# One 8-row share of two load and store steps moved from DMA engines 6 and 7 to engines 14 and 15, on GpSimd's queue

## The chip, the cores and the metric

The kernel runs on one core of a Trainium2 chip. The metric is the device time of one execution in microseconds (us). Beside it there is a profile of one execution, with its trace: every instruction of the engines PE (TensorE), DVE (VectorE), ACT (ScalarE), POOL (GpSimd) and SP (SyncE), and every packet that the core's 16 DMA engines moved.

## The reference

The input x has the shape (1, 512, 512, 192) in bfloat16: 262,144 pixels of 192 channels. The channels form 4 groups of 48. The reference pads by k // 2, and k is 1, so there is no padding and the loop has one step:

```python
for i in range(k):
    for j in range(k):
        out = out + jnp.einsum('bhwgc,gcd->bhwgd', xg[:, i:i+H, j:j+W, :, :], w[i, j])
```

So each pixel's 48 channels of a group are multiplied by that group's 48 x 48 matrix. It is a 1x1 grouped convolution. Input and output have 100.66 MB each.

## The kernel before, in words

**Pieces.** The pixels are cut into pieces that each lie over the 128 partitions (rows) of the SBUF tensor `ring`. A full piece has `BIG` = 104 pixels (columns) in each of the 128 rows: 104 x 192 x 2 = 39,936 bytes in a row, contiguous in DRAM. `ring` has five slots of 104 columns. Slot 0 first takes four short pieces (`HEAD`, 8 to 32 columns). `plan_pieces` puts two *shared* pieces (`SHARED`) among the full ones, after five and after ten of them. A piece is loaded into its slot, computed, written back into the same place, and stored from there.

**Shared pieces.** A full piece is one DMA, whose 128 rows go to all 16 engines, 8 rows each. A shared piece is 72 columns wide, does not use all rows, and is made of *shares*, each a block of rows with its own DMA. The tuple of a share is (first row, rows, parts, columns, queue): `parts` is the outer size that the DRAM side of its DMA shows (`transfers`), and so the number of DMA engines that take part, with 4 rows each. Before, there are three shares:

- rows 0 to 31, 41 columns, 8 parts, by SP's (load) and ACT's (store) queue: engines 0 to 7
- rows 32 to 47, 72 columns, 4 parts, by the same queues: engines 0 to 3
- rows 52 to 95, 72 columns, 11 parts, by GpSimd's queue both ways: engines 5 to 15

A row of 41 columns has 15,744 bytes, one of 72 columns 27,648. All rows of the piece are computed on, also those that were not loaded; only the shares are stored.

**The cursor.** The two queues of SP and ACT begin each DMA at engine 0. In GpSimd's queue a DMA over fewer than 16 engines goes on at the engine after the last one used. So `pool_dmas` issues, ahead of each 11-part transfer, a small DMA over 5 engines into the scratch tensor `cur` (5 rows of 2 x 32 elements), so that the 11 parts fall on engines 5 to 15 and the turn ends at engine 16, which is 0.

**Order of the work.** There is no scheduler; every engine's program is written out by hand.

- SP issues all loads in order of the pieces. `wait_slot` makes it wait, before a load into a slot, until the stores of the piece five slots back have landed, those of ACT's queue (`st_sem`) and those of GpSimd's (`ps_sem`).
- PE takes groups of 4 columns (`columns(g)`), 526 in all, two to a pair: 12 transposes of 128 x 128 per pair into PSUM (`xT_ps`, L247), and 6 matmuls per group against the block matrix `wt` into `o_ps` (L262). Before the first group of a piece it waits for its load, of both queues.
- DVE copies the transposed pair to SBUF (L286). ACT copies each group's result from PSUM back into `ring` (L304), and issues a piece's stores when it has copied the first group behind it (`store`, L298). The last pieces are stored in parts.
- POOL builds the identity and selection matrices at the start. After that it only handles the two shared pieces: wait for the slot, cursor and load (L197, L199), wait for ACT to have finished the piece, cursor and store (L197, L199).

Of the kernel before, what the change touches and what calls it, by code (L numbers as in the profile page):

```python
# [6 lines left out]
BF16 = mybir.dt.bfloat16  # L7
# [23 lines left out]
SHARED_AT = (5, 11)  # L31
SHARED_COLS = 72
SYNC, POOL = 0, 1
SHARED = ((0, 32, 8, 41, SYNC), (32, 16, 4, SHARED_COLS, SYNC), (52, 44, 11, SHARED_COLS, POOL))
CURSOR = 5
NXP = 4
NXS = 3
NOB = 4
# [38 lines left out]
def plan_pieces(npix):  # L77
    few = sum(rows * cols for _, rows, _, cols, _ in SHARED)
    at = list(SHARED_AT)
    if npix < len(at) * few + 128 * (sum(HEAD) + BIG * (at[-1] + 2)):  # L80
        at = []
    cols = (npix - few * len(at)) // 128
    assert cols % 4 == 0
    head = list(HEAD) if cols >= sum(HEAD) + BIG else []
    mid = cols - sum(head)
    slots = [[(BIG, None)]] * (mid // BIG) + ([[(mid % BIG, None)]] if mid % BIG else [])
    for i in at:
        slots.insert(i, [(SHARED_COLS, SHARED)])
    if head:
        slots.insert(0, [(s, None) for s in head])  # L90
    pieces, g, pix = [], 0, 0
    for n, parts in enumerate(slots):
        c = n * BIG % RCOLS
        for s, shares in parts:
            pieces.append(Piece(len(pieces), n, c, g, s, shares, pix))
            c, g, pix = c + s, pieces[-1].g1, pieces[-1].pix_end
    assert pix == npix
    return pieces


def bass_standalone__grouped__vision_kernel(nc, x, w, out):
# [10 lines left out]
    xf = x.rearrange("b h w c -> (b h w) c")  # L112
# [6 lines left out]
    def transfers(ap, ring, p, queue, c0=0, c1=None):  # L119
        for b in p.on(queue):  # L120
            px = ap[b.pix:b.pix + b.rows * b.cols, :]
            e0, e1 = c0, min(c1 or b.cols, b.cols)
            if b.parts == 1:
                view = px.rearrange("(p i) n -> p (i n)", p=b.rows)[:, e0 * C:e1 * C]
            else:
                view = px.rearrange("(c a i) n -> a c (i n)", a=b.parts, c=b.rows // b.parts)
            yield view, ring[b.r0:b.r0 + b.rows, (p.at + e0) * C:(p.at + e1) * C]
# [10 lines left out]
    pooled = [p for p in pieces if p.on(POOL)]  # L138
    pool_val = {p: 16 * len(p.on(POOL)) for p in pooled}

    with ExitStack() as es:
        block = es.enter_context(nc.Block())
        ring = es.enter_context(nc.sbuf_tensor("ring", [128, RCOLS * C], BF16))
# [8 lines left out]
        def sem(name):  # L152
            return es.enter_context(nc.semaphore(name))
# [3 lines left out]
        pl_sem = {p: sem(f"pl{p.i}") for p in pooled}  # L157
        ps_sem = {p: sem(f"ps{p.i}") for p in pooled}
        cur_sem = sem("cur_sem")
        cur = es.enter_context(nc.sbuf_tensor("cur", [CURSOR, 2 * len(pooled), 2, 32], BF16))  # L160
        w_sem, id_sem, e_sem, wb_sem, wc_sem = (sem(s) for s in ("w_sem", "id_sem", "e_sem", "wb_sem", "wc_sem"))
        p0_sem, p1_sem = sem("p0_sem"), sem("p1_sem")
        t_done, mm_done = sem("t_done"), sem("mm_done")
# [7 lines left out]
        def wait_slot(wq, p):  # L171
            for q in pieces:
                if q.slot == p.slot - RCOLS // BIG:
                    wq.wait(st_sem[q.i], st_val[q])
                    if q in pl_sem:
                        wq.wait(ps_sem[q], pool_val[q])

        @block.gpsimd
        def _(gp):
            wq = Waiter(gp)  # L180
            gp.memset(esel[:], 1.0).then_inc(p0_sem, 1)  # L181
            gp.memset(ident[:], 1.0).then_inc(p1_sem, 1)  # L182
            gp.wait_ge(p0_sem, 1)
            gp.affine_select(out=esel[:], in_=esel[:], pattern=[[-1, ECOLS]],  # L184
                             compare_op=AluOpType.is_equal, fill=0.0, base=ESHIFT,
                             channel_multiplier=1).then_inc(e_sem, 1)
            gp.wait_ge(p1_sem, 1)
            gp.affine_select(out=ident[:], in_=ident[:], pattern=[[-1, 128]],  # L188
                             compare_op=AluOpType.is_equal, fill=0.0, base=0,
                             channel_multiplier=1).then_inc(id_sem, 1)  # L190
            turns = [0]

            def pool_dmas(p, ap, inward, done):
                for dram, sbuf in transfers(ap, ring, p, POOL):
                    n = turns[0]
                    few = xf[0:CURSOR, 0:128].rearrange("p (a b) -> p a b", a=2)[:, :, 0:32]
                    gp.dma_start(cur[:, n], few).then_inc(cur_sem, 16)  # L197
                    turns[0] += 1
                    gp.dma_start(*((sbuf, dram) if inward else (dram, sbuf))).then_inc(done, 16)  # L199

            for p in pooled:
                wait_slot(wq, p)
                pool_dmas(p, xf, True, pl_sem[p])
                wq.wait(fa_done, p.g1)
                pool_dmas(p, of, False, ps_sem[p])
            for p in pooled:
                wq.wait(ps_sem[p], pool_val[p])
            wq.wait(cur_sem, 16 * turns[0])
# [130 lines left out]
```

## Time and profile before

| | |
|---|---|
| runs | 486.94, 486.96, 487.05 us; median 486.96 |
| profiled execution, its time | 486.76 us |
| its span, first to last instruction | 485.0 us |
| PE / ACT / DVE / POOL busy | 436.1 / 396.6 / 252.6 / 5.9 us |
| granted TensorE clock, mean | 0.957 |
| DMA moved | 202.24 MB, 417 GB/s |
| GpSimd's shared loads, issue to landing | 24.3 us (median of 2) |
| GpSimd's shared stores, issue to landing | 26.5 us (median of 2) |

The span is 1.8 us shorter than the execution's time. Busy times are sums over the span, so an engine that is busy 90% can still wait for another. In the profile's list of DMA queues q1 is SP's queue (loads), q10 ACT's (stores), q0 GpSimd's, and q8 and q14 bring instructions from DRAM. The share of a queue is the time that its packets took, as a share of 16 engines' span.

### The profile page before, as it was taken

How to read it: one execution, taken by the hardware profiler on the slowest of the kernel's cores; microseconds unless marked ns; L12 is line 12 of the kernel's file. 1: busy time of each engine (PE TensorE's matmuls, PEld its weight loads, DVE VectorE, ACT ScalarE, POOL GpSimd, SP SyncE). 2: the span in 40 equal slices, each digit the busy share in tenths (PEclk: the TensorE clock that was granted, in tenths of full speed). 3: DMA queues.
4: the chain of work that ended last, by engine and by line, in shares of the span. 5: the costliest groups of instructions: out<-in, count | busy, mean ns of one | idle time of the engine just before them, and what ended most of it. 6: DMA issues, size and time to landing. Idle time of an engine off the chain costs nothing.

```text
span 485.0 us, 14084 instructions
## 1 busy us (share of the span) xinstructions
PE 436.1 (90%) x6322; PEld 397.3 (82%) x6322; DVE 252.6 (52%) x264; ACT 396.6 (82%) x527; POOL 5.9 (1%) x16
## 2 busy tenths in 40 slices
PE   5979999999998999699859998999999999999910
PEld 5878889889888988688859897898888899889800
DVE  2535555565655555255525654655655556565500
ACT  3949999999998999499848997999989999999920
POOL 1000000100000000000000000000000000000000
PEclk9979999999999999799979999999999999999965
DMA  8999999999999999999999999999999999999993
GB/s 325 443 440 409 426 447 408 397 428 433 433 421 449 408 430 437 441 424 420 431 439 419 427 428 421 420 422 421 428 430 417 430 432 421 430 421 431 422 423 151
DMA packets 8443, 202.24 MB, mean 417 GB/s; under 512 B 1361, under 2 KB 1361, under 8 KB 2001
## 3 DMA queue, kind: packets, MB, share of 16 engines
q1 hardware_dynamic: 3496, 98.25, 47.6%
q10 hardware_dynamic: 4440, 98.23, 47.6%
q0 software_dynamic: 448, 4.87, 2.4%
q8 instruction: 50, 0.82, 0.6%
q14 instruction: 9, 0.07, 0.0%
HBM read 100.68 MB, written 100.66 MB: 415 GB/s over the span
## 4 chain that ended last, share of the span: by engine, by line
PE 70%; DMA 22%; issue 1%; another core or an unknown queue 1%; ACT 1%; ACTq 0%; SPq 0%
PE o_ps L262 41%; PE xT_ps L247 29%; DMA ring<-in_x_dram 13%; DMA out_dram<-ring 9%; ACT ring L304 1%; ACTq L298 0%; SPq L217 0%; SPq L213 0%
## 5 line engine op out<-in xcount | busy, mean ns | idle before, releaser
L304 ACT CAST ring<-o_ps 128x768 bf16<-128x768 f32 x526 | 395.3, 802 | 66.4 <-PE o_ps L262 57.4
L286 DVE COPY xT_sb<-xT_ps 128x1536 bf16<-128x1536 bf16 x263 | 252.0, 958 | 205.3 <-PE xT_ps L247 205.3
L262 PE MATMUL o_ps<-wt,xT_sb 128*128 128x144 bf16 (+1 forms) x3156 | 295.6, 236 | 9.7 <-ACT ring L304 3.9
L262 PEld LDWEIGHTS o_ps<-wt,xT_sb 128*128 128x128 bf16 x3156 | 214.6, 99 | 47.2 <-ACT ring L304 33.7
L247 PE MATMUL xT_ps<-ident,ring 128*128 128x128 bf16 x3156 | 224.6, 222 | 14.3 <-DMA ring<-in_x_dram 14.2
L247 PEld LDWEIGHTS xT_ps<-ident,ring 128*128 128x128 bf16 x3156 | 193.7, 99 | 15.5 <-DMA ring<-in_x_dram 12.5
L197 POOL DMA_DIRECT2D cur<-in_x_dram x4 | 2.3, 584 | 286.3 <-DMA out_dram<-ring 160.0
L230 PE MATMUL o_ps<-w_sb,esel 48*128 48x48 bf16 x10 | 0.6, 209 | 2.8 <-DMA w_sb<-in_w_dram 2.8
L230 PEld LDWEIGHTS o_ps<-w_sb,esel 48*128 48x128 bf16 x10 | 0.5, 111 | 2.8 <-issue 2.8
L280 DVE CAST wt<-o_ps 128x480 bf16<-128x480 f32 x1 | 0.7, 657 | 3.4 <-PE o_ps L230 3.4
L304 ACT ACT_TABLE_LOAD x1 | 1.3, 1283 | 0.8 <-PEq L324 0.8
L199 POOL DMA_DIRECT2D ring<-in_x_dram x2 | 1.1, 564 | 0.0
L199 POOL DMA_DIRECT2D out_dram<-ring x2 | 1.1, 559 | 0.0
L184 POOL TENSOR_SCALAR_AFFINE_SELECT esel<-esel 48x272 bf16<-48x272 bf16 x1 | 0.4, 402 | 0.0
L181 POOL MEMSET esel<- 48x272 bf16 x1 | 0.3, 318 | 0.3 <-POOLq L324 0.3
L188 POOL TENSOR_SCALAR_AFFINE_SELECT ident<-ident 128x128 bf16<-128x128 bf16 x1 | 0.3, 283 | 0.0
L182 POOL MEMSET ident<- 128x128 bf16 x1 | 0.2, 197 | 0.0
L324 POOL MEMSET const-float32-0.0<- 128x1 f32 x1 | 0.1, 98 | 0.3 <-issue 0.3
L324 POOL MEMSET const-bfloat16-1.0<- 128x1 bf16 x1 | 0.1, 101 | 0.0
L324 POOL MEMSET const-uint8-127<- 128x1 uint8 x1 | 0.1, 101 | 0.0
L324 POOL MEMSET const-float32-1.0<- 128x1 f32 x1 | 0.1, 98 | 0.0
## 6 DMA issues: line engine op xcount, KB each, us to landing
ring<-in_x_dram SPq DMA_DIRECT2D x18, 4992.0 KB, 35.0
out_dram<-ring ACTq DMA_DIRECT2D x12, 4992.0 KB, 42.8
out_dram<-ring ACTq DMA_DIRECT2D x10, 2496.0 KB, 47.3
out_dram<-ring ACTq DMA_DIRECT2D x3, 1536.0 KB, 21.2
ring<-in_x_dram POOLq DMA_DIRECT2D x2, 1188.0 KB, 24.3
out_dram<-ring POOLq DMA_DIRECT2D x2, 1188.0 KB, 26.5
ring<-in_x_dram SPq DMA_DIRECT2D x1, 1536.0 KB, 11.2
ring<-in_x_dram SPq DMA_DIRECT2D x1, 1344.0 KB, 8.1
```

The lines of the kernel that those rows point to most:

```text
L181: gp.memset(esel[:], 1.0).then_inc(p0_sem, 1)
L184: gp.affine_select(out=esel[:], in_=esel[:], pattern=[[-1, ECOLS]], compare_op=AluOpType.is_equal, fill=0.0, base=ESHIFT, channel_multipli ...
L188: gp.affine_select(out=ident[:], in_=ident[:], pattern=[[-1, 128]], compare_op=AluOpType.is_equal, fill=0.0, base=0, channel_multiplier=1) ...
L197: gp.dma_start(cur[:, n], few).then_inc(cur_sem, 16)
L199: gp.dma_start(*((sbuf, dram) if inward else (dram, sbuf))).then_inc(done, 16)
L230: last = pe.matmul(o_ps[:, NOB - 1, col:col + CG], lhsT=esel[:, s0:s0 + 128], rhs=w_sb[:, g, :], start=True, stop=True, skip_group_check=True)
L247: last = pe.transpose(xT_ps[:, g % NXP, j * 128:(j + 1) * 128], xg[:, j * 128:(j + 1) * 128], ident[:])
L262: last = pe.matmul(o_ps[:, v % NOB, c0_:c1_], lhsT=xs[:, j * 128:(j + 1) * 128], rhs=wt[:, WOFF[tc]:WOFF[tc] + (c1_ - c0_)], start=(tc == ...
L280: dve.tensor_copy(wt[:], o_ps[:, NOB - 1, 0:WCOLS]).then_inc(wc_sem, 1)
L286: dve.tensor_copy(xT_sb[pair % NXS][:, 0:n * 2 * UC].rearrange("p (g c) -> p g c", g=n), xT_ps[:, b0:b0 + n, 0:2 * UC]).then_inc(e_done, 1)
L304: act.copy(dst, o_ps[:, v % NOB:v % NOB + 2, 0:UC]).then_inc(fa_done, 1)
L324: nc = _bacc.Bacc("TRN2", target_bir_lowering=False, num_devices=1)
```

## The change

The share of rows 0 to 31 becomes one of rows 0 to 23 in 6 parts, on engines 0 to 5. A fourth share takes 8 rows of 41 columns in rows 120 to 127, in 2 parts, by GpSimd's queue. The numbers of pixels, of columns and of all other pieces stay the same; PE, DVE and ACT have the same instructions, with other rows in ACT's store of that share. POOL issues, for each shared load and each shared store, two more DMAs: a cursor over 14 engines (16 less the parts), and the eight rows, which then fall on engines 14 and 15. `cur` gets 16 rows, and a place for each of the eight turns.

```diff
-SHARED = ((0, 32, 8, 41, SYNC), (32, 16, 4, SHARED_COLS, SYNC), (52, 44, 11, SHARED_COLS, POOL))
-CURSOR = 5
+SHARED = ((0, 24, 6, 41, SYNC), (32, 16, 4, SHARED_COLS, SYNC),
+          (52, 44, 11, SHARED_COLS, POOL), (120, 8, 2, 41, POOL))
...
-        cur = es.enter_context(nc.sbuf_tensor("cur", [CURSOR, 2 * len(pooled), 2, 32], BF16))
+        turns_max = 2 * sum(len(p.on(POOL)) for p in pooled)
+        cur = es.enter_context(nc.sbuf_tensor("cur", [16, max(turns_max, 1), 2, 32], BF16))
...
             def pool_dmas(p, ap, inward, done):
-                for dram, sbuf in transfers(ap, ring, p, POOL):
+                for b, (dram, sbuf) in zip(p.on(POOL), transfers(ap, ring, p, POOL)):
                     n = turns[0]
-                    few = xf[0:CURSOR, 0:128].rearrange("p (a b) -> p a b", a=2)[:, :, 0:32]
-                    gp.dma_start(cur[:, n], few).then_inc(cur_sem, 16)
+                    r = 16 - b.parts
+                    few = xf[0:r, 0:128].rearrange("p (a b) -> p a b", a=2)[:, :, 0:32]
+                    gp.dma_start(cur[0:r, n], few).then_inc(cur_sem, 16)
                     turns[0] += 1
                     gp.dma_start(*((sbuf, dram) if inward else (dram, sbuf))).then_inc(done, 16)
```

## The prediction

> **What bounds the kernel now.** I read the page first: who is busy, the DMA row, the DMA queues.
>
> ```profile
> PE 436.1 (90%) x6322; PEld 397.3 (82%) x6322; DVE 252.6 (52%) x264; ACT 396.6 (82%) x527; POOL 5.9 (1%) x16
> DMA  8999999999999999999999999999999999999993
> q1 hardware_dynamic: 3496, 98.25, 47.6%
> q10 hardware_dynamic: 4440, 98.23, 47.6%
> q0 software_dynamic: 448, 4.87, 2.4%
> q8 instruction: 50, 0.82, 0.6%
> ```
>
> PE is busy 90%, but the queues' shares add to 47.6 + 47.6 + 2.4 + 0.6 = 98.2% of sixteen DMA engines over the whole span: on average an engine is free for 1.8% of 485.0, 8.7 us. I looked at the stages next, to see where those 8.7 us lie (columns: stretch, its length, busy time of each engine, granted clock, DMA share, GB/s).
>
> ```profile
> 232.00:332.00 100.00, 90.64 (x1309) 82.73 (x1308) 52.39 (x55) 81.87 (x109) 1.10 (x2) 0.97 1.00 425
> 332.00:434.00 102.00, 100.77 (x1499) 91.58 (x1497) 59.39 (x62) 93.41 (x126) 0.00 (x0) 1.00 1.00 426
> 434.00:464.00 30.00, 28.09 (x412) 25.06 (x409) 16.29 (x17) 27.44 (x37) 0.00 (x0) 1.00 1.00 426
> 464.00:472.00 8.00, 0.00 (x0) 0.00 (x0) 0.00 (x0) 0.00 (x0) 0.00 (x0) 0.51 0.99 421
> 472.00:476.00 4.00, 0.00 (x0) 0.00 (x0) 0.00 (x0) 0.00 (x0) 0.00 (x0) 0.50 0.79 334
> 476.00:480.00 4.00, 0.00 (x0) 0.00 (x0) 0.00 (x0) 0.00 (x0) 0.00 (x0) 0.50 0.30 127
> 480.00:484.00 4.00, 0.00 (x0) 0.00 (x0) 0.00 (x0) 0.00 (x0) 0.00 (x0) 0.50 0.19 81
> ```
>
> Computing ends at 464, and the DMA engines are full from 28 to 472. Only then does the share fall: from 480 to 484 it is 0.19, three engines of sixteen. So the end is set by the last DMA engine to work off its own list, and what counts is each engine's list.
>
> The trace lists every DMA packet with queue, start, duration and size, but not its engine. I put them in sixteen **lanes**: under load a packet starts 3 or 4 ns before the one ahead of it ends, and each lane must hold, queue by queue, the list that the kernel gives one engine. The lists differ: engines 0 to 3 have 15,744-byte and 27,648-byte packets on SP's and ACT's queues (q1, q10), 4 alone carries no 27,648, 5 to 7 have 15,744 and GpSimd's (q0) 27,648, 8 to 15 GpSimd's alone. All packets fit. The end of each lane (us):
>
> ```
> engines 0-3           476.4 476.5 482.4 483.4   (the late two: four 8 KB packets of q14 each)
> engine 4              477.5
> engine 5              475.2
> engines 6, 7          483.3 483.9               (six 16 KB packets of q8 each)
> engines 8-13          474.4 474.8 475.3 475.6 476.6 477.1   (q8, six or seven each)
> engines 14, 15        472.0 472.2               (no q8, no q14)
> ```
>
> Their mean is 477.3. The last semaphore write comes at 484.2, the span ends at 485.0, and the execution's time is 486.76; the median of the runs is 486.96, 0.20 above. A us off the last lane is a us off all of these.
>
> Two readings in this table are mine. The q8 packets (instructions) go round eight lanes, two of the group 5 to 7, then six of the group 8 to 15; eight neighbours in that order can only be 6 to 13, so 6 and 7 are the late two, and 14 and 15 the ones without. And one lane has its stores stretched, a 39,936-byte packet taking 1,476 + about 110 ns, from 71 to 464 us. Up to 316 it is engine 4's, since its stretched packets include stores of 15,744 bytes; at 315 three lanes ran dry together (0.5 to 1.4 us), and behind that I give the stretched lane to engine 4 again, by the stretch alone.
>
> **Part by part.** *Moved bytes.* Four transfers (load and store of two pieces) shift 8 rows of 41 columns from engines 6 and 7 to 14 and 15: per transfer and engine four packets of 15,744 bytes at 587 ns, 2.35 us; over four transfers 16 x 587 = 9.39 us. Engines 6 and 7: 483.3 and 483.9 become 473.9 and 474.5. Engines 14 and 15: 472.0 and 472.2 become 481.4 and 481.6. Engines 0 to 5 keep their rows. As lanes are full to their end, these sums hold one for one; 14 and 15 were dry for 0.5 and 0.7 us at 315, which the new work would fill, so 480.9 is their lower end.
>
> *Now last* is an engine of 0 to 3, at 483.4. That is the price of cover gone: 9.4 us come off the last engine, but the next stands only 0.5 us ahead.
>
> *GpSimd's new DMAs.* Eight more instructions: per shared transfer a cursor DMA on 14 engines (0.55 us on POOL, from the rows of L197) and the eight rows (0.56, L199). POOL's queue holds nothing else until the next shared piece (it idles 286 us ahead of L197), so 1.1 us more per transfer there costs nothing by itself. The packets do: from the lanes of now, an engine that takes no part in a cursor or a transfer of this queue still runs an 8-byte packet, or four of 4 bytes, and each has a 4-byte one behind, 6 to 9 ns net apiece. New on engines 0 to 3: about 7 such per transfer, 28 in all, 0.17 to 0.25 us; I take 0.2. So 483.4 becomes 483.6.
>
> *When the moved shares land.* GpSimd's packets take turns with the other queues of their engine. The first shared load ends on lanes 14 and 15 at 113; four more turns of 1,476 + 587 ns (load queue empty then) and 1.1 us for the issue give 123; PE starts on that piece at about 139.7, where the store of the piece before is issued: 17 us to spare. The second: 250 plus four turns of 2 x 1,476 + 587 = 264 + 1.1, needed at 276.9: 12 to spare. Below that cover each us late would be a us of PE, which has over 6 us of stored work ahead of it at the end (464 against 472 less the last store's 8 x 234 ns). The moved store of the first piece ends at 178 + 14 + 1 = 193. SP's load of the slot waits for it and for ACT's store of that piece, which landed at 198.5, last on engine 7; without 6 and 7 that comes at 193 too. So the load's wait ends no later than now, and PE's stall behind it (5.0 us near 250) can only shrink; that is worth nothing at the end, as the lanes are full anyway.
>
> *Sum.* Last lane 483.88 to 483.6: 0.3 us less. 486.76 becomes 486.5 for the profiled execution, 486.96 becomes **486.7** for the median.
>
> [...] On lanes 14 and 15 GpSimd's packets of 27,648 bytes take 1,025 ns, as they do on engine 5, and the one stretched lane is engine 4's. [...]
>
> **Rivals.** *The stretch on engines 2 and 3 goes (faster).* The late two of 0 to 3 lost 2.9 and 2.8 us between 268 and 307, where their store packets took 1,476 + about 290 ns, and the other two lanes' did not. Nothing like it happened to them before or after, so it is no part of their list. If it does not come back, they end at 479.7 and 480.8, engines 14 and 15 are last with 481.6, and the time falls by 2.3 to 484.7 (484.0 with the 480.9 above). For it: it depends on how transfers meet, and all of that shifts after 96 us. Against it: these two lanes' own list is unchanged.
>
> *The stretch grows (slower).* The same mechanism on the same engines over twice as many packets: 483.6 + 2.8 = 486.4, up 2.5, 489.5. It decides from 1.3 us more on, since 484.85 is the edge of no change. Against: the three runs agree within 0.11 us, so it was never past engine 7's 483.9 in them.
>
> *The slow lane is 14 or 15 (slower).* If behind 316 us the stretched lane, at 477.5, was one of 14 and 15, that one ends at 477.5 + 9.39 = 486.9: up 3.0, 489.9. Against it stand the 15,744-byte packets above. [...]
>
> *The rows do not go to 14 and 15 (slower).* The 44 rows of before went to eleven lanes with four packets each, but eight rows by GpSimd's queue are not in the trace. Spread one row to each of engines 0 to 7, every one of them gets a packet of 587 ns in four transfers, 2.35 us: 483.6 + 2.35 = 485.9, up 2.1, 489.0. [...]
>
> **How the numbers follow.** 0.2% of 486.96, 0.97 us, is about what a measurement of this kernel tells from no change. Forecast (an engine of 0 to 3 last near 483.6): 0.38, own range 486.0 to 487.9. Stretch gone, wholly or by over half a us: 0.38. Stretch grown: 0.11. Slow lane at 14 or 15: 0.07. Rows elsewhere: 0.06. So faster 0.38, same 0.38, slower 0.24. The range goes from 484.0, the lower end of the faster case, to 489.0, which leaves out the two dearest cases, somewhat under 0.2 in all.
>
> **What would show it.** Right: 48 packets of 15,744 bytes on q1 and on q10 (64 each now) and 32 on q0; the DMA share still 1.00 up to 472; the share from 476 to 482 higher than now, as 14 and 15 run there, and gone by 483.6; 6 and 7 done by 475; the last lane one with q14. The wait of SP near 198 shorter. Wrong: fewer than 32 such packets on q0 or other sizes; a last lane at 485 or more without q8 and q14; PE idle for DMA by over 6 us more than its 14.2; a DMA share under 1.00 before 464.

## The result

| | before | changed |
|---|---|---|
| runs, us | 486.76 to 487.05 (4) | 488.31, 489.01, 489.65, 489.85 |
| median, us | 486.95 | 489.33 |
| ratio | | 1.0047, 95% interval 1.0029 to 1.0065 |
| profiled execution, us | 486.76 | 488.31 |
| span, us | 485.0 | 486.6 |

The changed kernel is slower by 0.5%, 2.4 us in the medians. The forecast was no change, 486.7, with a range from 484.0 to 489.0. On some chips used for the experiments the kernel before itself varied by several us from run to run (486.5 to 494.9 on one), so each experiment is read against its own comparison and by its lanes.

The page of the changed kernel, the lines that answer to those of before (busy times, DMA share in 40 slices, DMA queues):

```profile
PE 436.2 (90%) x6322; PEld 396.9 (82%) x6322; DVE 252.5 (52%) x264; ACT 396.6 (81%) x527; POOL 10.3 (2%) x24
DMA  8999999999999999999999999999999999999992
q1 hardware_dynamic: 3476, 98.00, 47.3%
q10 hardware_dynamic: 4420, 97.98, 47.3%
q0 software_dynamic: 896, 5.38, 2.6%
q8 instruction: 50, 0.82, 0.6%
```

POOL has eight more DMAs, 4.4 us of it, beside everything else. 0.25 MB left each of q1 and q10, and q0 took 0.51 MB. The trace has 48 packets of 15,744 bytes on q1, 48 on q10 and 32 on q0, each of the 32 at 587 ns. So the rows moved as written.

The stages of the changed kernel (stretch, length, busy time of each engine, granted clock, DMA share, GB/s):

```profile
332.00:434.00 102.00, 100.59 (x1491) 91.21 (x1488) 59.51 (x63) 93.16 (x125) 0.00 (x0) 1.00 1.00 429
434.00:464.00 30.00, 29.63 (x439) 26.83 (x438) 17.83 (x19) 27.56 (x37) 0.00 (x0) 1.00 0.99 420
464.00:472.00 8.00, 1.20 (x13) 0.78 (x12) 0.00 (x0) 2.44 (x4) 0.00 (x0) 0.73 1.01 429
472.00:476.00 4.00, 0.00 (x0) 0.00 (x0) 0.00 (x0) 0.00 (x0) 0.00 (x0) 0.50 0.89 375
476.00:480.00 4.00, 0.00 (x0) 0.00 (x0) 0.00 (x0) 0.00 (x0) 0.00 (x0) 0.50 0.28 119
480.00:484.00 4.00, 0.00 (x0) 0.00 (x0) 0.00 (x0) 0.00 (x0) 0.00 (x0) 0.50 0.12 51
484.00:486.00 2.00, 0.00 (x0) 0.00 (x0) 0.00 (x0) 0.00 (x0) 0.00 (x0) 0.50 0.07 28
```

The engines are full until 472, as before. From 472 to 476 more of them work than before (0.89 for 0.79). From 480 on there are fewer, 0.12 for 0.19, two of sixteen, but they go on past 484. The work is more even but for two engines, and those are later than any was before.

The packets put on sixteen lanes, as in the prediction (end in us):

```
                      before                    changed
engines 0-3           476.4 476.5 482.4 483.4   476.2 476.2 479.1 479.7
engine 4              477.5                     479.1 or 473.8
engine 5              483.9 or 483.3            484.7   (six q8 packets)
engines 14, 15        (not told apart)          485.4 (seven q8 packets), 475.0 (none)
engines 6-13          (not told apart)          473.8 475.5 475.5 475.8 476.0 476.0 476.8 (one of them engine 6), and the other of 473.8 and 479.1
```

In the changed kernel engine 5 alone has rows on SP's queue and GpSimd's 27,648-byte packets, and 14 and 15 alone have 15,744-byte packets on q0, so these lanes have names. Engine 5 brings instructions (q8) and has not been relieved. One of 14 and 15 brings instructions too and got 9.4 us more (16 packets at 587 ns). These two are the ones past 484. Engine 4's lane is not told apart from one of 6 to 13 (479.1 or 473.8). The step from the last lane to the execution's time is 2.9 us in both profiles: 483.9 to 486.76, and 485.4 to 488.31.

### The profile page after: what moved, and what is told of

Read it like the earlier page. It is cut to its first block, busy times and chain, and to the rows that moved or that the text cites. A ratio compares the mean times of both kernels' runs of the same rounds, so it can differ in the third digit from the quotient of the medians.

```text
span 486.6 us, 14092 instructions
## 1 busy us (share of the span) xinstructions
PE 436.2 (90%) x6322; PEld 396.9 (82%) x6322; DVE 252.5 (52%) x264; ACT 396.6 (81%) x527; POOL 10.3 (2%) x24
## 4 chain that ended last, share of the span: by engine, by line
PE 48%; DMA 38%; another core or an unknown queue 8%; ACT 1%; issue 1%; SPq 1%; POOL 0%
PE o_ps L264 28%; PE xT_ps L249 20%; DMA ring<-in_x_dram 19%; DMA out_dram<-ring 18%; ACT ring L306 1%; SPq L219 0%; POOL cur L199 0%; POOL out_dram L201 0%; SPq L215 0%; SPq L51 0%
## 5 line engine op out<-in xcount | busy, mean ns | idle before, releaser
L249 PE MATMUL xT_ps<-ident,ring 128*128 128x128 bf16 x3156 | 224.9, 223 | 19.5 <-DMA ring<-in_x_dram 19.4
L199 POOL DMA_DIRECT2D cur<-in_x_dram x8 | 4.5, 564 | 286.3 <-DMA out_dram<-ring 159.3
L201 POOL DMA_DIRECT2D ring<-in_x_dram x4 | 2.3, 568 | 0.0
L201 POOL DMA_DIRECT2D out_dram<-ring x4 | 2.3, 564 | 0.0
```

What stands on the lines that cost most here:

```text
L199: gp.dma_start(cur[0:r, n], few).then_inc(cur_sem, 16)
L249: last = pe.transpose(xT_ps[:, g % NXP, j * 128:(j + 1) * 128], xg[:, j * 128:(j + 1) * 128], ident[:])
```

## The experiments

The theories: **A**, the lists of the lanes: engine 5, the last, was not relieved, and a loaded one of 14 and 15 became last. **B**, the prediction's reading, 6 and 7 were last. **C**, GpSimd's additional DMAs cost the time. **D** came up on the way: a late landing of GpSimd's store.

**Numbers for the lanes.** GpSimd issues tiny DMAs over 2, 14, 3, 13, ... engines, 23 at the start and 23 behind the second shared piece. An engine that takes part in one runs a 32-byte packet, the others an 8-byte one, as before the four cursors over 5 engines left 20 packets of 128 bytes and 44 of 8. Together with a lane's list of transfers, this row of packets names each lane (0 and 1 share one). The names rest on the turn through the engines that the kernel's cursor counts on; the lists that follow from it fit the packets of before, such as q0's 176 of 27,648 bytes: eleven lanes, four in each of the four transfers.

```diff
+LABELS = (2, 14, 3, 13, 6, 10, 7, 9, 9, 7, 10, 6, 11, 5, 12, 4, 13, 3, 14, 2, 15, 3, 14)
...
+            def label():
+                for r in LABELS:
...
+                    gp.dma_start(cur[0:r, turns[0]], few).then_inc(cur_sem, 16)
```

> The kernel before, with 23 tiny GpSimd DMAs over 2 to 15 engines at the start and again after the second shared piece, so that every DMA engine has a list of small packets of its own and each lane of the trace can be given its number. Theory A (engine 5 and one of 14 and 15 bring instructions, so the change left the last engine as it was and put 9.4 us on a loaded one): the eight lanes with 16 KB q8 packets are 5, one of 6 and 7, five of 8 to 13, and one of 14 and 15; engine 5 ends last, near 484. Theory B (the reading of the prediction): they are 6 to 13, and 6 and 7 end last. Theory C (GpSimd's additional DMAs and the later landing of its shares cost the time, wherever the rows are) says nothing of the lanes. All: time 487 to 488 us, as 46 tiny DMAs add up to 0.8 us to each engine's list.

Measured: 487.63. The second row of labels, read lane by lane:

```
engine   0|1 480.1   0|1 483.4 (q14)   2 480.4   3 480.0 (q14)   4 479.7 or 477.7 (stores stretched)
q8       5 484.8   6 484.7   9, 10, 11, 12 475.0 to 476.8   13 477.7 or 479.7   14 476.9
no q8    7 476.8   8 471.7   15 471.0
```

The eight engines with instructions are 5, 6 and 9 to 14. Theory B is wrong by its identification: engine 7 is free, 5 is not, 14 is not. The trace does not fix which of the ends 477.7 and 479.7 is that of 4 and which that of 13. The q8 packets begin at 13 and go on with 14, 5, 6, 9. In the changed kernel, too, 14 or 15 has the second packet and 5 the third. The same order in the kernel before gives its lanes their names: 13 ended at 476.6, 14 at 477.1, 5 at 483.9 and 6 at 483.3, so engine 5 was the last.

**The rows left out.** The changed kernel without the fourth share; its pixels are not moved at all.

```diff
-                for b, (dram, sbuf) in zip(p.on(POOL), transfers(ap, ring, p, POOL)):
+                for b, (dram, sbuf) in zip(p.on(POOL)[:1], transfers(ap, ring, p, POOL)):
```

> The changed kernel without the share of rows 120 to 127: its pixels are neither loaded nor stored (4 x 126 KB less in all), its cursor DMAs are gone too. Engines 6 and 7 have 9.4 us less to move than in the kernel before, all others the same. Theory A: engine 5 is still last near 483.9, so the time is that of the kernel before, 486.4 to 487.5. Theory B: the last are engines of 0 to 3, 479.7 to 483.4, so 482.8 to 486.5. Theory C: 487 or less, as GpSimd issues what it issued before.

Measured: 486.83 against 486.86, ratio 0.9997 (0.9988 to 1.0005). Half a MB less to move and no gain. Lane 5 ends at 484.3 and 6 at 473.9; the tail of its stages:

```profile
476.00:480.00 4.00, 0.00 (x0) 0.00 (x0) 0.00 (x0) 0.00 (x0) 0.00 (x0) 0.50 0.22 93
480.00:484.00 4.00, 0.00 (x0) 0.00 (x0) 0.00 (x0) 0.00 (x0) 0.00 (x0) 0.50 0.12 51
484.00:488.00 4.00, 0.00 (x0) 0.00 (x0) 0.00 (x0) 0.00 (x0) 0.00 (x0) 0.57 0.01 4
```

The share from 480 to 484 fell from 0.19 to 0.12, by the one engine relieved, and the end stayed. Taking 9.4 us from 6 and 7 was worth nothing while 5 stood (484.3).

**The same rows by GpSimd's queue, without a change of engine.** The edit is to the changed kernel.

```diff
-          (52, 44, 11, SHARED_COLS, POOL), (120, 8, 2, 41, POOL))
+          (52, 44, 11, SHARED_COLS, POOL), (24, 8, 2, 41, POOL))
...
+                    first = 6 if b.parts == 2 else 5
+                    cursor(first)
                     gp.dma_start(*((sbuf, dram) if inward else (dram, sbuf))).then_inc(done, 16)
+                    cursor(16 - first - b.parts)
```

> The changed kernel with the fourth share in rows 24 to 31, that is on engines 6 and 7 where the kernel before has it, still by GpSimd's queue, with a cursor DMA ahead (6 engines) and one behind (8 engines). Each engine moves the bytes that it moves in the kernel before. Theory A: as before, 486.7 to 487.7 (0.3 us for the small packets). Theory C: 489 or more, since GpSimd issues 12 DMAs more than before where the change issues 8.

Measured: 488.42 (486.84 to 492.03), ratio 1.0029 (1.0007 to 1.0051). This stands against A as expected: the profiled execution, 486.84 with lane 5 last at 484.0, fits A, but the median does not, and no profile of a later execution was taken. It made theory C worth testing by itself.

**Only the additional DMAs.** The kernel before, with cursors over 14 and 2 engines behind each of GpSimd's transfers.

```diff
                     gp.dma_start(*((sbuf, dram) if inward else (dram, sbuf))).then_inc(done, 16)
+                    cursor(14)
+                    cursor(2)
```

> The kernel before, with a cursor DMA over 14 engines and one over 2 behind each of GpSimd's four transfers: as many DMAs more as the change has (8), with no rows moved to another engine. Theory A: 0.1 to 0.3 us for the small packets, 486.9 to 487.2. Theory C: most of the loss, 488.4 or more.

Measured: 487.24, ratio 0.9990 (0.9974 to 1.0005). Eight more DMAs without data cost nothing that can be told. C in its plain form is out; that moving the rows by GpSimd's queue costs something by itself is not.

**Which pair gets the rows.** The kernel of the same rows by GpSimd's queue, with `first = 7` for engines 7 and 8, or rows 112 to 119 and `first = 12` for 12 and 13. GpSimd issues the same number of DMAs in both.

> The eight rows of 41 columns go by GpSimd's queue (cursor 7, rows 24 to 31, cursor 7) to engines 7 and 8, which the labels show without instruction packets; engine 6 has 9.4 us less than in the kernel before. GpSimd issues the same 12 DMAs more as when the rows went to engines 6 and 7. Theory A (the pair decides: engine 5 is last and unrelieved, and 14 brings instructions): 7 or 8 end at 475 to 482, engine 5 still last near 484, 486.5 to 487.5. Theory C (GpSimd's DMAs cost it, wherever the rows are): 488 to 489.5, as the median of 488.4 with the rows on 6 and 7.

> The same with rows 112 to 119 on engines 12 and 13 (cursor 12, rows, cursor 2), both of which bring instructions and end at 475 to 477 in the kernel before. Theory A: 475 to 477 + 9.4 = 484.4 to 486.5, up 0.5 to 2.6 on the last lane, 487.5 to 489.6. Theory C: 488 to 489.5, the same as with the rows on 7 and 8; so the two runs together tell the theories apart.

> The changed kernel once more, beside these runs on one chip. Theory A: engine 14 (477.1 + 9.4) last, 488.3 to 489.9, and a second profile with lane 14 at 485 to 486.5. Theory C: the same time, with the lane of no matter.

Measured, all on the chip where the kernel before ran from 486.5 to 494.9: 7 and 8 489.86, ratio 1.0016 (0.9987 to 1.0044); 12 and 13 490.01, 1.0026 (1.0004 to 1.0047); the changed kernel 489.28, 1.0011 (0.9990 to 1.0033). The ratios tell little here; the fastest executions go the way of A (486.47 before, 487.29 with 7 and 8, 488.35 changed, 488.72 with 12 and 13). The lanes tell more: with 7 and 8 the last one ended at 485.1, 12 and 13 ended at 487.4 and 487.8, and in the second profile of the changed kernel lane 14 was last with 486.4, by the sum 477.1 + 9.4 = 486.5; 486.4 + 2.9 is its 489.26. The two pairs again on another chip:

> The kernel with the rows on engines 7 and 8 again, on another chip: on the last one the kernel before itself ran from 486.5 to 494.9, so its comparison told nothing. Theory A: 486.5 to 487.7. Theory C: 488 to 489.5.

> The kernel with the rows on engines 12 and 13 again, beside the one on 7 and 8: GpSimd's work is the same, the engines alone differ. Theory A: lanes 12 and 13 end at 486 to 488 (487.4 and 487.8 in the profile of the run before), 488.7 to 490. Theory C: within 0.3 us of the run on 7 and 8.

Measured: 7 and 8 487.72, ratio 0.9998 (0.9977 to 1.0018); 12 and 13 490.52, ratio 1.0050 (1.0027 to 1.0073). The intervals do not meet, and GpSimd issues the same in both, so C does not explain the difference. The tails, first with 7 and 8, then with 12 and 13:

```profile
480.00:484.00 4.00, 0.00 (x0) 0.00 (x0) 0.00 (x0) 0.00 (x0) 0.00 (x0) 0.50 0.16 67
484.00:488.00 4.00, 0.00 (x0) 0.00 (x0) 0.00 (x0) 0.00 (x0) 0.00 (x0) 0.62 0.01 2
```

```profile
480.00:484.00 4.00, 0.00 (x0) 0.00 (x0) 0.00 (x0) 0.00 (x0) 0.00 (x0) 0.50 0.23 99
484.00:488.00 4.00, 0.00 (x0) 0.00 (x0) 0.00 (x0) 0.00 (x0) 0.00 (x0) 0.50 0.13 55
```

A share of 0.13 from 484 to 488 is the work of two engines of sixteen. Lanes 12 and 13 ended at 487.0 and 489.9, and a third lane at 485.8. With the rows on 7 and 8 the last are 5 and one of 0 to 3, at 483.8 and 483.7.

**List or late store.** The chain of waits of the changed kernel has an entry that before did not (start, us, what):

```profile
296.70 46.95 DMA out_dram<-ring
343.72 35.16 DMA ring<-in_x_dram
```

GpSimd's store of the moved rows of the second piece landed at 343.7, and SP's load into that slot started only then; before, it started at 330.6. PE's waits for loads rose from 14.2 to 19.4 us. That is theory D: the late landing, not the list. One profile on record speaks against it: with the rows on 6 and 7 by GpSimd's queue, SP's load started at 339.4 and PE's waits for loads were 18.8 us, yet that execution took 486.84. The kernels with 7 and 8 (load at 332.2) and with 12 and 13 (346.1) do not tell the two apart. First, the eight rows on 7 and 8, with GpSimd's second store held back:

```diff
+                    if b.parts == 2 and not inward and p is pooled[-1]:
+                        wq.wait(fa_done, p.g1 + 16)
```

> The kernel with the rows on engines 7 and 8, whose GpSimd also waits for 16 more groups of ACT (13 us) before it stores the eight rows of the second shared piece. The slot's load then starts near 345 instead of 332, as in the changed kernel, with no busy engine loaded. Theory A (engine 14's list): as without the delay, 486.5 to 487.8. Theory D (the late landing): 488.3 to 489.5, as the changed kernel.

Measured: 487.13, ratio 1.0004 (0.9994 to 1.0014), but the run missed its aim: issued at 309.0 instead of 293.0, the store still landed at 332.6, 23.6 us behind its issue where it had been 39.2. It says nothing on D. Second, lane 14 loaded and no store changed:

```diff
+                    if inward:
+                        px = ap[p.blocks[0].pix:p.blocks[0].pix + 8 * 82, :]
+                        cursor(14)
+                        gp.dma_start(ring[120:128, p.at * C:(p.at + 82) * C],
+                                     px.rearrange("(c a i) n -> a c (i n)", a=2, c=4)).then_inc(done, 16)
```

> The kernel before, plus a GpSimd load per shared piece of 8 rows of 82 columns into rows 120 to 127, which no store reads (its rows are additional work, 0.5 MB in all), on engines 14 and 15: 16 packets / 2 x 31,488 bytes, twice 4.66 us = 9.3 us more on each, the sum that the change puts there. All stores stay as before, so the slot's load starts near 331. Theory A: lane 14 ends at 477.1 + 9.3 = 486.4, 488.8 to 489.8. Theory D: 486.7 to 487.8.

Measured: 488.52, ratio 1.0034 (1.0021 to 1.0048), lane 14 last with 485.6; 485.6 + 2.9 is the 488.46 of its profile:

```profile
480.00:484.00 4.00, 0.00 (x0) 0.00 (x0) 0.00 (x0) 0.00 (x0) 0.00 (x0) 0.50 0.18 75
484.00:488.00 4.00, 0.00 (x0) 0.00 (x0) 0.00 (x0) 0.00 (x0) 0.00 (x0) 0.50 0.04 14
```

SP's load into the slot started at 329.4, so there was no late store. PE waits for the additional load too (18.5 us for loads in all), but its work still ended well ahead of the last lane, by 472. So a longer list on 14 costs 1.6 us, of the 2.4 that the changed kernel lost; D is not needed for that part. Whether D adds something in some executions is open: in both profiles of the changed kernel lane 14 is never dry for more than 0.25 us behind the first 10 us, so there it does not. The control:

> The same additional load on engines 7 and 8 (cursors 7 and 7). Theory A: 7 ends at 475.2 + 9.3 = 484.5 at most and 8 below, about level with engine 5: 486.7 to 487.7. If the additional load costs time wherever it runs, 488.8 to 489.8.

Measured: 491.97, ratio 1.0109 (1.0084 to 1.0134), the slowest of all and against both expectations. Lane 7 was last with 488.8 instead of 484.5. Its added packets, and far more those of 8, took 1,166 to 1,893 ns, where the same packets on 14 and 15 all took 1,166; lane 14's own loads were stretched at the same times (543 to 755 ns at 125, 254 and 257 us). One reading is that 7 and 8 wrote rows that 14 and 15 were writing at the same time. The trace does not show a packet's rows and no run took the overlap away, so the cause stays open, and as a control this run fails. That an additional load costs time wherever it runs is therefore not excluded by it; against that stand the lanes, since in each of the two runs a loaded lane was last.

**Better shares.** If the lanes' lists set the end, shares fitted to the lists must gain. A first try takes 5, 6 and 7 out of SP's share and spreads their rows over 8 to 15:

```diff
+SHARED = ((0, 20, 5, 40, SYNC), (32, 16, 4, SHARED_COLS, SYNC),
+          (52, 44, 11, SHARED_COLS, POOL), (96, 32, 8, 16, POOL))
```

> The first share becomes 20 rows of 40 columns in 5 parts (engines 0 to 4), and the fourth 32 rows of 16 columns in rows 96 to 127 by GpSimd's queue (engines 8 to 15, 8-engine cursor). Engines 5, 6 and 7 lose 9.4 us each, engines 8 to 15 gain 16 packets of 6,144 bytes at 234 ns, 3.7 us each. Theory A: 5, 6 and 7 end by 474.5, the loaded one of 14 and 15 at 477.1 + 3.7 = 480.9, the two of 0 to 3 with q14 at 479.5 to 483.2, so 484.0 to 486.3. Theory B: the loaded ones of 8 to 13 end at 480.8, the same 484.0 to 486.3, so this run does not tell A from B. Theory C: 489 or more, as GpSimd moves more rows than in the changed kernel.

Measured: 486.58 (484.64 to 487.42), ratio 0.9978 (0.9965 to 0.9992). Lanes 5 to 7 ended at 471.8 to 475.4 and the loaded 14 at 480.8, as expected; in the profile the two of 0 to 3 with q14 were last with 482.2 and 484.2, their stores stretched again between 250 and 310. The second try also relieves those, with no additional DMA:

```diff
-SHARED_COLS = 72
+SHARED_COLS = 88
-SHARED = ((0, 32, 8, 41, SYNC), (32, 16, 4, SHARED_COLS, SYNC), (52, 44, 11, SHARED_COLS, POOL))
+SHARED = ((0, 20, 5, 40, SYNC), (32, 16, 4, 60, SYNC), (52, 44, 11, SHARED_COLS, POOL))
```

> The kernel before with shares cut to the lanes: 20 rows of 40 columns (engines 0 to 4), 16 rows of 60 (0 to 3), and 44 rows of 88 by GpSimd (5 to 15): 5,632 pixels as before, the same number of DMAs of GpSimd as before. One column of four rows costs an engine 0.227 us over the four transfers. Theory A: engines 5 and 6 come to 478, 9 to 14 to 478 to 481, the two of 0 to 3 with q14 to 476.5 to 480.5, so the last lane is 480 to 481 and the time 483.3 to 484.5. PE computes four groups more per shared piece (8 x 0.82 = 6.5 us), hidden as long as the lanes are behind it. Theory C: no more DMAs of GpSimd, so no change: 486.5 to 487.

Measured: 483.52 (483.33 to 483.89, 6 runs). Its ratio of 0.9908 (0.9883 to 0.9933) is against a kernel before that varied on that chip; against about 486.9 (the kernel before had 486.95, 486.86 and 486.97 in other sets of runs, and 487.81 in one) it is 0.993. All lanes end between 474.5 and 480.9, and the tail shows it:

```profile
472.00:476.00 4.00, 0.00 (x0) 0.00 (x0) 0.00 (x0) 0.00 (x0) 0.00 (x0) 0.50 0.89 378
476.00:480.00 4.00, 0.00 (x0) 0.00 (x0) 0.00 (x0) 0.00 (x0) 0.00 (x0) 0.50 0.41 172
480.00:484.00 4.00, 0.00 (x0) 0.00 (x0) 0.00 (x0) 0.00 (x0) 0.00 (x0) 0.51 0.01 5
```

After 480 almost nothing is left to move. PE's eight more groups are hidden. One step further, with 32, 81 and 84 columns:

> The rebalanced kernel with 20 rows of 32 columns, 16 rows of 81 and 44 rows of 84. Its first version ended with engine 4 at 480.9 and 14 at 480.2. Theory A: engine 4 comes to 480.9 - 8 x 0.227 = 479.1, 14 to 480.2 - 4 x 0.227 = 479.3, the two of 0 to 3 with q14 to 476.3 + 13 x 0.227 = 479.3: 481.8 to 482.3. If the stretch of up to 3 us on those two comes back, 484 to 485. Theory C: as the first version, 483.5.

Measured: 484.72 (482.96 to 488.64), ratio 0.9934 (0.9910 to 0.9958). The profiled execution, 483.78, has one of 0 to 3 last with 481.1, its stores stretched as before. The step gives 0 to 3 more, and so less room for that. The two rebalanced kernels ran on different chips and their intervals overlap, so which is faster is not shown: the second had the fastest execution (482.96 for 483.33), the first the narrower spread. Both have a median below that of the first try.

## Why the prediction was wrong

**The model held.** Lanes full to their end (a DMA share of 1.00 up to 464, before), the last one sets the time: the last lane and the execution's time differ by 2.9 us in the profiles of before, of the changed kernel twice, of the pair on 12 and 13 (489.9, 492.8) and of the loaded 14 and 15.

**The step that failed** is in the table of lanes: "eight neighbours in that order can only be 6 to 13, so 6 and 7 are the late two, and 14 and 15 the ones without". The trace gave two of the group 5 to 7 and six of 8 to 15, ascending. That they are neighbours was put in by hand; they are 5, 6 and 9 to 14. From it the sums for the lanes fail one after the other. Engine 5, last with 483.9, kept its rows. Engine 7, which had been early, lost 9.4 us that nobody waited for. Engine 14 ended at 477.1, not 472, and 477.1 + 9.4 = 486.5 is about what it reached (485.4 and 486.4 in two profiles). With the names right, the same sum gives 483.9 to 486.5, 2.6 us more, 489.6; 489.33 was measured.

**The term of 9.39 us** was about right for 14 (8.3 and 9.3). For 15 it shows in part only: 475.0 and 476.4 for 471 to 472. Before, that lane ran ahead of the others and its packets took 6 to 8 us longer than their usual time; in the changed kernel 1.4 us. So the prediction's "these sums hold one for one" failed for this lane, which was ahead of the others; why its packets took longer is open.

**GpSimd's DMAs** at 0.2 us: not more than that, by the kernel with cursors only.

**The landing of the moved shares** was worked out on lanes 8 and 15, which I took for 14 and 15. The first store landed at 202.6 instead of 193, the second at 343.7, and SP's load waited for them, 4 and 13 us longer, where I had it wait less. PE's additional 5.2 us stayed just below the 6 that the lanes' lead covers.

**The rivals.** "The stretch on engines 2 and 3 goes" happened (479.1 and 479.7), and bought nothing, as 5 and 14 were behind it (484.7 and 485.4); what sets the stretch off, no run shows. The labels also give these two as 3 and one of 0 and 1. "The slow lane is 14 or 15" gave 489.9, close to what came by luck, since the cause is another: not the stretched lane, which is engine 4's by the labels, but the one with instructions. Its chance of 0.07 was too low, since the identification that it hung on rested on an order alone. "The rows do not go to 14 and 15" is out by the packets: the 32 of 15,744 bytes on q0 lie on two lanes. Its spread of one row to each of engines 0 to 7, 2.35 us, was an assumption that no run shows.

**The engines without instructions**, 7, 8 and 15 of those from 5 on, end by the labels at 476.8, 471.7 and 471.0, ahead of 5 and 6 with 484.8 and 484.7.

**Open:** why the rows on 6 and 7 by GpSimd's queue cost 0.3% in the median, and what made the kernel before vary on some chips.

## What to carry to other kernels

When transfers bound a kernel, ask for each DMA engine's own list, its instruction packets included, and move work only from the engine that ends last: here half a MB less on 6 and 7 gained nothing (ratio 0.9997), and shares fitted to the lists took 486.9 to 483.52. Give the lanes names before moving bytes between them: 46 tiny DMAs over different numbers of engines did it here in one execution of 487.63, 0.8 us above the 486.86 beside it, where the wrong move cost 2.4. A sum over lanes is no better than the name on each.

## What was not expected of the hardware

In this kernel instructions come on q8 in 16 KB packets, 50 from 16 to 459 us, about every 9 us, one engine after the other, by the labels on engines 5, 6 and 9 to 14. Whose they are is not shown; that they are PE's is an estimate from the page, where PE has 12,644 instructions, its weight loads included, and DVE and ACT have 791. Each costs its engine about 1.3 us (0.95 for itself, 0.4 more for the packet behind it, in the trace of before), six or seven per engine, 8 to 9 us in all: as much as the 9.4 us of rows that the change moved. Beside engine 5's 484.8, engine 7 with the same list of rows ended at 476.8.
